# Query, key and value projections on scaled fp16 halves instead of float32r halves, in a gated mix of memory attention and a SiLU feed-forward

## The chip, the cores and the metric

The kernel runs on one core of one Trainium2 chip (trn2). The metric is the device time of one launch in microseconds (us); lower is better. Runs of one kernel are compared on the same chip.

## What is computed

`x` has 2048 rows of 448 features. Block A is attention with 16 heads of 28 features in four segments of 512 rows; each segment attends within itself and also reads a running memory of the earlier segments. Block B is a feed-forward of 1792 inner features. A gate per row mixes the two.

```python
q, k, v = x @ wq, x @ wk, x @ wv            # heads of 28, segments of 512 rows
phi = lambda t: where(t > 0, t + 1, exp(t))
for s in range(4):
    logits = qs @ ks.T * 28 ** -0.5 + mask  # masked where key > query: -1e9
    a_dot = softmax(logits) @ vs
    a_mem = (phi(qs) @ M) / (phi(qs) @ z + 1e-6)
    o[s] = g * a_mem + (1 - g) * a_dot      # g = sigmoid(beta), one per head
    M, z = M + phi(ks).T @ vs, z + phi(ks).sum()
a = o @ wo
b = silu(x @ w1) @ w2
out = sigmoid(x . gate_w) * a + (1 - sigmoid(x . gate_w)) * b
```

## The kernel before, in words

**Two parts for each number.** TensorE multiplies fewer bits than a float32 has, so each operand is split into a high part and a low remainder, and a product is the sum of high*high, high*low and low*high. `passes` lists these: 448 features are three chunks of 128 and a last one of 64, whose low part is packed beside the high, so 3*3 + 2 = 11 matmuls make one product. `product` (L547, matmuls at L555) runs them in groups of 3, 3, 3 and 2, one per chunk, into one PSUM bank. The q and k products of a segment and a group of four heads (`proj`, 16 of each) are 11 matmuls of 128x512; `vproj` (16, one per 128 rows) is 11 matmuls of 128x450 (448 and a column for the gate). That makes 176 matmuls for each of q, k and v.

**Which parts.** Before, q, k and v use float32r parts: the high part is a rounded copy (ScalarE, L770, L786, L810), the low part a plain subtraction (VectorE or GpSimd, L774, L791, L813). They need no scale. The feed-forward uses fp16 parts (`halves`, L512: ScalarE at L515, VectorE at L507), and these need a power-of-two scale, since fp16 has a small exponent range. So `x` is loaded twice: into `xraw` for the projections, whose float32r parts `xT` live in two buffers, and later into `rawf`, from which `x16` (L523) makes the fp16 parts `xh` for the feed-forward, segment 0 within stage one and the other three in stage two.

**Scales.** `size` (L379, VectorE) takes the largest magnitude of a loaded piece per partition. `scales(a, b)` turns several of these into a scale: a reduction (`most`, L405), a TensorE transpose (L409), four small VectorE steps (L412 to L416), a TensorE broadcast (L418) and two more VectorE steps that give `up`, the scale, and `top`, its inverse (L422, L423). Before, scales were needed only behind the projections, at the eviction of PSUM: `sqk` and `sv` scale q, k and v into fp16 pairs (`stg`, L846, L848; `vt`, L902, L906).

**phi.** From the PSUM of `proj`: `pr` = relu(-q) on ScalarE (L862), `pe` = exp(-pr) on ScalarE (L864), `ph` = max(q, 0) + pe on VectorE (L865), which reads PSUM again. For q, `phq` splits it in two float32r parts (L869, L871); for k it is transposed (L882) and becomes `phk` (L885, L887). `memory` (L936, L938) and `retrieve` (L973, L974) are the running memory.

**Stages and order.** Stage one is `project()`: it loads `x` and the weights, makes q, k, v, the memory parts and the scales of everything. When it ends, its SBUF is given to stage two, where attention (`maxima`, L660 and L670; `attention`, L1216 to L1258) is interleaved with the feed-forward (L555 on `xh,wa`, L1095 to L1118). At the end the output projection (L555 on `wos,oT`) is added.

No order is written out by hand. A list scheduler (`Sched`) holds a cost for each task, adds a hop time when a result goes from one engine to another (`HOP`), and in each step starts the task that can begin first; among equals the priority decides. What it settles is a fixed order per engine: each engine executes its own queue strictly in that order, and an instruction whose input is late holds up all behind it. Tasks with two possible engines (`either`, `scaled`) go to VectorE or GpSimd by their costs. All DMAs are issued from SP. PSUM has three banks for projections and feed-forward (`mm`), three for scores and v (`sc`) and two others (`cc`). `WARM` = 15 matmuls on a constant run first, while the first data is loaded.

Of the kernel before, what the change touches and what calls it, by code (L numbers as in the profile page):

```python
# [8 lines left out]
F32 = mybir.dt.float32  # L9
# [26 lines left out]
WARM = 15  # L36
BANKS = {"mm": 3, "sc": 3, "cc": 2}
# [7 lines left out]
WOT = 30.0  # L45
TUS = 1.6
TLAT = 4.0
SLACK = 0.75
LOP = 14.63
LATE = 0.08  # L50
FIRST = 120.0
WPRIO = 120.0
# [4 lines left out]
MP = 14.75  # L57
VF = 2.5
VA = 1.36
VS = 6.77  # L60
NV = 8
XS0 = 2.29
VC = -7.5
OT1 = 6.44
XS = 4.78
QS = -4.81
KS1 = -3.68
SS = -1.76
# [6 lines left out]
PRICE = 27.28  # L75
PVRUNS = [((1, 0), 1)]
PVP = 45.81
FLO = -17.93
FHI = 690.04
WOP = 96.32  # L80
SZ = 26.65
SZSTEP = 1.85
XPRIO = 81.97
WBP = -7.77
# [23 lines left out]
class Sched:  # L108
# [3 lines left out]
    HOP = {"PE": 0.2, "ACT": 0.145, "DVE": 0.13, "POOL": 0.1, "SP": 0.1}  # L112
# [124 lines left out]
def infini_mix(ctx: ExitStack, tc: tile.TileContext, x, wq, wk, wv, wo, beta, w1, w2, out):  # L237
# [67 lines left out]
    def scaled(cols, fn, *deps, **k):  # L305
        eng = {"DVE": nc.vector, "POOL": nc.gpsimd}
        return sch.add(("DVE", "POOL"), (0.07 + 0.00104 * cols, 0.2 + 0.0042 * cols), lambda e: fn(eng[e]), deps, port=True, **k)
# [35 lines left out]
    own2 = const.tile([128, 2], F32, name="own2")  # L343
    upw = const.tile([128, 3], F32, name="upw")
    sqk = const.tile([128, 2 * NSEG], F32, name="sqk")
# [4 lines left out]
    sv = const.tile([128, NSEG], F32, name="sv")  # L350
# [7 lines left out]
    X16 = {0: base.tile([128, 7, L], F16, name="xh0")}  # L358
# [11 lines left out]
    SIZE, SCALED, XH = {}, {}, {}  # L370

    def size(j, view, n, *deps, uses=(), prio):
# [8 lines left out]
        SIZE[j].append(dve(n, go, *deps, uses=uses, prio=prio))  # L381

# [7 lines left out]
    def scales(a, b, prio):  # L390
# [5 lines left out]
        wide1 = a <= W1 < b  # L396

        def m1():
            if wide1:
                for j in range(a, b):  # L400
                    nc.vector.tensor_reduce(most[:, j:j + 1], sizes[:, cols[j][0]:cols[j][1]], axis=AX.X, op=OP.max)
                for j in (HQ, HK):
                    nc.vector.tensor_max(most[:, W1:W1 + 1], most[:, W1:W1 + 1], most[:, j:j + 1])
            else:
                nc.vector.tensor_reduce(most[:, a:b], sizes[:, cols[a][0]:cols[b - 1][1]].rearrange("p (j n) -> p j n", j=n),  # L405
                                        axis=AX.X, op=OP.max)
        t = dve(500 if wide1 else 130, m1, *[d for j in range(a, b) for d in SIZE[j]],
                *([SCALED[HQ], SCALED[HK]] if wide1 else []), prio=prio)
# [114 lines left out]
    def x16(s, prio, *deps):  # L523
# [4 lines left out]
        for c in range(4):  # L528
            r = Buf(RAW)
            d = dma(262e3, lambda c=c, r=r: start(r.v, x[s, :, c]), *deps, takes=[r], prio=prio + 0.01 * c)  # L530
            if s == 0:
# [5 lines left out]
                def src(r=r):  # L537
                    return r.v.rearrange("p (c n) -> p c n", c=4)
# [867 lines left out]
```

## Time and profile before

| what | value |
|---|---|
| time, median of 3 runs | 576.42 us (575.96 to 577.6) |
| span of the profiled execution | 574.4 us |
| what lies around that span, against the median | 2.0 us |
| instructions | 11662 |
| TensorE busy | 556.2 us (97%), 4055 matmuls |
| VectorE busy | 426.7 us (74%) |
| ScalarE busy | 398.7 us (69%) |
| GpSimd busy | 346.3 us (60%) |
| DMA | 83.14 MB, mean 145 GB/s |
| mean granted TensorE clock | 0.991 |

The profile lists no time of its own for the profiled execution beside its span, so the 2.0 us between span and median are taken as a constant around it. A matmul's duration in the profile is its way through the array; matmuls overlap, so the rate is read from how far apart they start, and TensorE's 97% is not 97% of its peak.

### The profile page before, as it was taken

The numbers are of one execution on the slowest core, as the hardware profiler recorded it, in microseconds if no ns is written. First come the engines' busy times: TensorE is split into PE (matmuls) and PEld (weight loads), VectorE is DVE, ScalarE is ACT, GpSimd is POOL, SyncE is SP. The second block draws the span as 40 slices with busy tenths as digits, with TensorE's granted clock in tenths as the row PEclk, the third lists the DMA queues.
The fourth block names the chain that finished last, engine by engine and source line by source line (L and its number), as shares of the span: only waits on it lengthen the run. The fifth ranks groups of instructions, "written<-read, shape, count | busy, mean of one in ns | idle before, by whom it ended". The sixth has DMA issues, their size and how long they took to land.

```text
span 574.4 us, 11662 instructions
## 1 busy us (share of the span) xinstructions
PE 556.2 (97%) x4055; PEld 346.0 (60%) x4055; DVE 426.7 (74%) x1104; ACT 398.7 (69%) x695; POOL 346.3 (60%) x489
## 2 busy tenths in 40 slices
PE   9899999999998999999999999999999999999997
PEld 5587877888854455555565555555555654544544
DVE  7898889779877996578865688777996327555634
ACT  7568878566558788799977799967999846142321
POOL 5803626534324579999978899887999971131300
PEclk9899999999999799999999999999999999999999
DMA  8577875435747444344313433245330237888521
GB/s 302 181 231 224 249 206 168 130 99 165 238 127 199 127 144 146 98 119 109 96 53 110 136 104 99 64 154 141 109 87 4 64 113 242 209 235 236 130 77 65
DMA packets 80363, 83.14 MB, mean 145 GB/s; under 512 B 44296, under 2 KB 67976, under 8 KB 80304
## 3 DMA queue, kind: packets, MB, share of 16 engines
q1 hardware_dynamic: 80304, 82.39, 48.7%
q8 instruction: 32, 0.52, 0.4%
q14 instruction: 27, 0.22, 0.1%
HBM read 52.60 MB, written 26.09 MB: 137 GB/s over the span
## 4 chain that ended last, share of the span: by engine, by line
PE 56%; DVE 17%; ACT 10%; POOL 7%; DMA 5%; issue 5%; SPq 0%; DVEq 0%; ACTq 0%; POOLq 0%
PE mm L555 19%; PE mm L1118 16%; PE sc L555 8%; POOL phl L1237 4%; PE sc L1216 4%; PE sc L660 3%; DVE sc L670 3%; PE cc L1250 3%; ACT pf L1221 3%; DMA rawf<-in_w_dram 3%; ACT phl L1233 2%; DVE stg L848 2%; DVE ph L865 1%; DVE sizes L379 1%; DVE xh L507 1%
## 5 line engine op out<-in xcount | busy, mean ns | idle before, releaser
L1237 POOL TENSOR_TENSOR phl<-pf,phl 128x384 f16<-128x384 f32 (+1 forms) x192 | 190.2, 1013 | 12.2 <-ACT phl L1233 11.8
L1118 PE MATMUL mm<-wb,ghl 128*128 128x448 f16 (+1 forms) x684 | 143.4, 349 | 1.0 <-DVE ghl L1101 0.8
L555 PE MATMUL mm<-xh,wa 128*128 128x512 f16 x572 | 141.7, 379 | 0.5 <-DVE ghl L1101 0.4
L670 DVE CUSTOM_DVE_ANT_0 sc<-sc,mk 128x384 f32<-128x384 f32 (+1 forms) x192 | 105.1, 569 | 33.3 <-PE sc L660 26.1
L1221 ACT ACTIVATE pf<-sc,es 128x512 f32<-128x512 f32 (+1 forms) x192 | 109.4, 621 | 19.7 <-PE sc L1216 16.0
L1118 PEld LDWEIGHTS <-ghl 128*128 128x128 f16 x684 | 65.2, 97 | 57.0 <-issue 3.1
L555 PEld LDWEIGHTS <-wa 128*128 128x128 f16 x572 | 54.5, 97 | 57.8 <-issue 4.0
L1233 ACT ACTIVATE phl<-pf 128x1280 f16<-128x1280 f32 x64 | 81.5, 1275 | 10.7 <-POOL pf L1227 10.2
L660 PE MATMUL sc<-ring 84*128 84x128 f16 (+3 forms) x256 | 59.2, 304 | 2.7 <-DVE mx L670 1.7
L1216 PE MATMUL sc<-ring 86*128 86x512 f16 (+3 forms) x256 | 58.8, 302 | 2.2 <-ACT pf L1221 1.0
L1095 ACT ACTIVATE th<-mm,ths 128x512 f32<-128x512 f32 x52 | 35.7, 691 | 33.3 <-PE mm L555 33.3
L1097 DVE SCALAR_TENSOR_TENSOR mm<-th,mm 128x512 f32<-128x512 f32 x52 | 36.4, 705 | 19.4 <-ACT th L1095 19.3
L555 PE MATMUL mm<-xT,wqs 128*128 128x512 f32 x176 | 48.2, 409 | 0.1
L1250 PEld LDWEIGHTS <-phl 128*128 128x128 f16 x1280 | 42.1, 97 | 10.0 <-issue 1.3
L555 PE MATMUL mm<-xT,wks 128*128 128x512 f32 x176 | 45.7, 401 | 0.0
L1258 DVE TENSOR_REDUCE oraw<-cc 128x116 f32<-128x232 f32 x64 | 25.0, 392 | 26.1 <-PE cc L1250 25.9
L1250 PE MATMUL cc<-vg,phl 128*128 128x29 f16 (+1 forms) x1280 | 44.0, 183 | 0.0
L566 POOL TENSOR_TENSOR ol<-ol,ml 128x448 f32<-128x448 f32 x12 | 14.2, 1180 | 48.2 <-DMA ol<-o_scr 29.0
L1101 DVE SCALAR_TENSOR_TENSOR ghl<-mm,ghl 128x512 f16<-128x512 f32 x52 | 35.5, 685 | 9.4 <-ACT ghl L1099 9.1
L555 PE MATMUL sc<-wvs,xT 128*128 128x450 f32 x176 | 40.4, 375 | 0.2 <-DVE wvs L813 0.2
L1216 PEld LDWEIGHTS <-ring 86*128 86x128 f16 x256 | 24.1, 98 | 23.3 <-issue 4.7
L1099 ACT ACTIVATE ghl<-mm 128x512 f16<-128x512 f32 x52 | 30.8, 599 | 9.6 <-DVE mm L1097 9.6
(163 smaller groups left out, 903.6 us busy)
## 6 DMA issues: line engine op xcount, KB each, us to landing
rawf<-in_w_dram SPq DMA_DIRECT2D x26, 256.0 KB
rawf<-in_w_dram SPq DMA_DIRECT2D x28, 224.0 KB
xraw<-in_x_dram SPq DMA_DIRECT2D x16, 256.0 KB
rawf<-in_x_dram SPq DMA_DIRECT2D x16, 256.0 KB
v_scr<-vt SPq DMA_DIRECT2D x16, 232.0 KB
vg<-v_scr SPq DMA_DIRECT2D x16, 232.0 KB
q_scr<-stg SPq DMA_DIRECT2D x16, 224.0 KB
k_scr<-stg SPq DMA_DIRECT2D x16, 224.0 KB
```

Source lines behind the costliest of these rows:

```text
L555: nc.tensor.matmul(ps(), *p[i], start=(i == 0), stop=(i == n - 1))
L660: nc.tensor.matmul(ps.v[:, u:u + n], rg.v[:KS, 0, hh, i * 128:(i + 1) * 128], rg.v[:KS, 1, hh, :n], start=(i > 0), stop=(i > 0 or j == 3), ...
L670: nc.vector.tensor_tensor_reduce(r, r, MK[:, L - n:], 1.0, NEG, OP.add, OP.max, mx.v[:, hh, i:i + 1])
L1095: e1 = sact(L, lambda ps=ps, th=th: nc.scalar.activation(th.v, ps.v, AF.Tanh, scale=ths[:, s:s + 1]), m, takes=[th], uses=[ps], prio=p0)
L1097: e2 = dve(L, lambda ps=ps, th=th: nc.vector.scalar_tensor_tensor(ps.v, th.v, 1.0, ps.v, op0=OP.add, op1=OP.mult), e1, uses=[ps, th], prio=p0)
L1101: e4 = dve(L, lambda ps=ps, g=g: nc.vector.scalar_tensor_tensor(g.v[:, 1], ps.v, DOWN, g.v[:, 0], op0=OP.mult, op1=OP.subtract), e3, uses= ...
L1118: nc.tensor.matmul(ps.v[:, lo:hi], g.v[:, y, sl], w.v[:, z, lo:hi], start=(j == 0 and i == 0), stop=(j == len(fs) - 1 and i == 2))
L1216: nc.tensor.matmul(ps.v[:, e:e + w], rg.v[:KK, 1, hh, j * 128:(j + 1) * 128], rg.v[:KK, 0, hh, j * 128:], start=True, stop=True)
L1221: ex.append(sact(e, lambda b=b, ps=ps, pf=pf, e=e: nc.scalar.activation(pf.v[:, b, :e], ps.v[:, :e], AF.Exp, scale=es[:, s:s + 1]), m, *ex ...
L1233: hi = copy(1280, lambda hl=hl, flat=flat: nc.scalar.activation(hl.v[:, 0], flat(), AF.Copy), *mk, takes=[hl], uses=[pf], prio=p0 + 2)
L1237: low = pool(w - u, lambda hl=hl, flat=flat, u=u, w=w: nc.gpsimd.tensor_sub(hl.v[:, 1, u:w], flat()[:, u:w], hl.v[:, 0, u:w]), low, uses=[ ...
L1250: nc.tensor.matmul(p[:, i, :2 - z], hl.v[:, z, u:u + 128], vg.v[:, j, hh, :2 - z], start=(z == zs[0] and i == 0), stop=(z == zs[-1] and j ...
```

## The change

The q, k and v projections now use the fp16 parts of the feed-forward, so the scales of `x`, `wv`, `wq` and `wk` are needed before the first product. The parts of `x` are made once, in stage one, for all four segments (`xhalves` into `X16`, now in the base pool), and the feed-forward reads them; `x16` and its loads are gone. The sizes of the weights are now sums of squares on ScalarE (`squares`), and their scale is a power of two near the root. The product comes out scaled, so q, k and v are evicted with one constant (`FIT`); phi gets its scale from `tqk` and `nqk`; `pp` = max(q, 0) is a VectorE step of its own that reads PSUM, and `ph` = pp + pe is now an addition from SBUF that may go to either VectorE or GpSimd. 16 further warm-up matmuls (`MORE` pairs) are spread between the first scales. The ring `xraw` grows from 6 to 8 buffers. Some thirty costs and priorities of the scheduler are set anew. The core of the diff:

```diff
+MORE = 8
+HPRIO = -3.02
+FIT = 2.0 ** -26
-SLACK = 0.75
-LOP = 14.63
+SLACK = 0.94
+LOP = 17.33
...
-    HOP = {"PE": 0.2, "ACT": 0.145, "DVE": 0.13, "POOL": 0.1, "SP": 0.1}
+    HOP = {"PE": 0.29, "ACT": 0.235, "DVE": 0.22, "POOL": 0.19, "SP": 0.19}
...
-    X16 = {0: base.tile([128, 7, L], F16, name="xh0")}
+    X16 = {s: base.tile([128, 7, L], F16, name=f"xh{s}") for s in range(NSEG)}
...
+    def squares(j, view, n, *deps, uses=(), prio):
...
+        SIZE[j].append(copy(n + 200, lambda: nc.scalar.activation(junk.v[:, :n], view(), AF.Square, accum_out=sizes[:, lo:lo + 1]),
...
+            if root:
+                nc.vector.tensor_scalar(few[:, 2:3].bitcast(I32), few[:, 1:2].bitcast(I32), 1, 0x3f800000,
+                                        op0=OP.logical_shift_right, op1=OP.bitwise_and)
...
+    def true(s, prio):
+        def go():
+            for i, j in enumerate((WQ, WK)):
+                nc.vector.tensor_scalar(tqk[:, 3 * s + i:3 * s + i + 1], top[:, j:j + 1], top[:, xi(s)], None, op0=OP.mult)
+            nc.vector.tensor_scalar(nqk[:, 3 * s:3 * s + 2], tqk[:, 3 * s:3 * s + 2], -1.0, None, op0=OP.mult)
...
-    def x16(s, prio, *deps):
...
-        XTR = cycle([wp.tile([128, 7, L], F32R, name=f"xT{i}") for i in range(2)])
-        W = {n: wp.tile([128, 8, D + 2 if n == "v" else L], F32R, name=f"w{n}s") for n in "qkv"}
+        W = {n: wp.tile([128, 8, D + 2 if n == "v" else L], F16, name=f"w{n}s") for n in "qkv"}
...
-        ring("xraw", [128, L], F32, 6)
+        ring("xraw", [128, L], F32, 8)
+        ring("pp", [GW, L], F32, 2)
...
+        for _ in range(MORE):
+            END1.append(pe(half(L, 2), lambda: [nc.tensor.matmul(
+                wb.v, maskb, maskb[:, None, :].to_broadcast([128, 4, 128]), start=True, stop=True) for _ in range(2)],
+                END1[-1], uses=[wb], prio=200))
...
-        def xquarter(tb, prio):
...
-        def xfeat(s, c, prio):
...
+        def xhalves(s, c, prio):
...
+            XC[s, c] = halves(NSEG - 1 - s, hi, lo, lambda: X16[s], src, L, d, prio, uses=[b])
+            XH.setdefault(s, []).extend(XC[s, c])
...
+                squares(j, v, n, d, uses=[b], prio=prio + 0.01 * c)
                 if name != "v":
...
+                    size(j + 1, lambda v=v: v().rearrange("p (g e) -> p g e", g=NG)[:, :, GW:], 64, d, uses=[b],
+                         prio=HPRIO + 0.01 * c)
...
+        def whalves(name, prio):
...
+                WS[name][c] = halves(j, (ALL, c), [((ALL, 4 + c), (ALL,), (ALL, c))], lambda: W[name], v, n, d, prio + 0.01 * c,
+                                     uses=[b], more=SIZE[j + 1][c:c + 1] if name != "v" else [])
...
-            p = product(lambda: ps.v, lambda: passes(w, XT[s].v), L, prio,
-                        deps={c: WS[which][c] + (XC[s, c] if s else XDONE[0]) for c in range(NC + 1)}, takes=[ps],
-                        uses=[XT[s]])
+            p = product(lambda: ps.v, lambda: passes(w, X16[s]), L, prio,
+                        deps={c: WS[which][c] + (XC[s, c] if s else XH[0]) for c in range(NC + 1)}, takes=[ps],
+                        kind=half)
...
-            hi = sact(L, lambda: nc.scalar.activation(hl.v[:, 0], ps.v, AF.Copy, scale=sqk[:, k:k + 1]), p,
-                     (QREADY if which == "q" else KREADY)[s], takes=[hl], uses=[ps], prio=prio)
+            hi = act(L, lambda: nc.scalar.activation(hl.v[:, 0], ps.v, AF.Copy, scale=FIT), p, takes=[hl], uses=[ps],
+                     prio=prio)
...
-            tp = dve(L, lambda: nc.vector.scalar_tensor_tensor(ph.v, ps.v[:GW], 0.0, e.v, op0=OP.max, op1=OP.add), te,
-                     takes=[ph], uses=[e, ps], prio=prio)
+            tu = dve(L, lambda: nc.vector.tensor_scalar(po.v, ps.v[:GW], tk, 0.0, op0=OP.mult, op1=OP.max), p, QREADY[s],
+                     takes=[po], uses=[ps], prio=prio)
+            te = copy(L + 65, lambda: nc.scalar.activation(e.v, r.v, AF.Exp, scale=nqk[:GW, k:k + 1]), tr, QREADY[s], takes=[e],
+                      uses=[r], prio=prio)
+            tp = either(L, lambda g: g.tensor_add(ph.v, po.v, e.v), te, tu, takes=[ph], uses=[e, po], prio=prio)
...
         for tb in range(TB):
-            load_x(0, tb, -9 + 0.01 * tb + (0.5 if tb else 0))
-        weight("v", wv, -8.9, places[:4])
+            load_x(0, tb, -12 + 0.01 * tb)
+        weight("v", wv, -11, places[:4])
+        weight("q", wq, -10, places[4:8])
+        weight("k", wk, -9, places[8:])
+        t_gh = gates()
+        scales(NSEG - 1, NSEG, -12)
         for tb in range(TB):
-            xquarter(tb, -9 + 0.01 * tb + (0.5 if tb else 0))
...
+            xhalves(0, tb, -11.5 + tb * 0.7 + (tb > 0))
+        scales(WV, WV + 1, -11)
+        whalves("v", -10.8)
+        scales(WQ, WQ + 1, QS)
+        whalves("q", QS + 0.1)
+        scales(WK, WK + 1, KS1)
+        whalves("k", KS1 + 0.1)
...
-            if s not in XH:
-                x16(s, prio(0) - XLEAD, *list(t1.values())[:1])
```

The retrieve products (L973, L974) keep their float32r parts. The size of the columns of `wq` and `wk` that hold a block of `w1` (`HQ`, `HK`) stays on VectorE, one small reduction for each loaded piece.

More of the change, by code (lines that the diff above doesn't have):

```diff
@@ L1044, in project @@
         END1.append(scales(W1, W2 + 1, WPRIO - 10))
-        x16(0, XPRIO, SCALED[W1])
-        END1.extend(XH[0])
+        for s in range(NSEG):
+            DER[s] = derive(s, XPRIO + s)
+            END1.append(DER[s])
         END1.extend(GDONE)
```

317 lines of the change are left out of this document (131 added, 186 removed).

## The prediction, made before the changed kernel ran

> **What bounds the kernel now.** I read the page first (span, busy shares, slices), then the busy times by stage, then the instructions in order of time and in groups.
>
> ```profile
> span 574.4 us, 11662 instructions
> PE 556.2 (97%) x4055; PEld 346.0 (60%) x4055; DVE 426.7 (74%) x1104; ACT 398.7 (69%) x695; POOL 346.3 (60%) x489
> PEclk9899999999999799999999999999999999999999
> ```
>
> TensorE (PE) is busy almost throughout, so a microsecond is won only if TensorE issues fewer or faster matmuls or waits less. The windows split this by stage (columns: length, busy time of PE, weight loads, VectorE, ScalarE, GpSimd, then granted clock, DMA share, GB/s):
>
> ```profile
> 0.00:6.00 6.00, 4.96 (x14) 1.88 (x15) 2.62 (x11) 3.27 (x5) 3.97 (x25) 1.00 0.66 211
> 6.00:14.00 8.00, 7.81 (x36) 6.20 (x35) 7.18 (x14) 6.45 (x12) 3.71 (x4) 1.00 1.01 367
> 14.00:18.60 4.60, 1.94 (x10) 1.29 (x9) 4.50 (x13) 2.81 (x8) 4.60 (x4) 1.00 0.77 261
> 18.60:22.10 3.50, 3.50 (x11) 2.33 (x10) 3.50 (x14) 1.62 (x4) 3.50 (x4) 0.51 0.65 227
> 22.10:30.00 7.90, 7.90 (x38) 6.20 (x37) 6.16 (x26) 4.06 (x10) 4.26 (x4) 1.00 0.37 124
> 30.00:60.00 30.00, 29.76 (x156) 24.69 (x155) 27.48 (x81) 23.78 (x54) 5.90 (x8) 1.00 0.80 237
> 60.00:163.60 103.60, 99.78 (x560) 83.08 (x559) 87.92 (x216) 72.35 (x157) 45.50 (x74) 1.00 0.58 172
> 163.60:200.00 36.40, 34.10 (x192) 16.50 (x192) 31.48 (x86) 26.03 (x43) 15.27 (x21) 0.91 0.55 154
> 200.00:570.00 370.00, 365.81 (x3048) 203.44 (x3047) 255.09 (x649) 258.35 (x410) 259.62 (x350) 1.00 0.42 122
> ```
>
> Stage one ends at 163.6. From 30 on TensorE stands idle only 0.24 + 3.82 = 4.1 us of it; in the change of stage 2.3; in the remaining 370 us 4.2. The clock of 0.91 there is about 6.6 us at half rate (0.09 * 36.4 / 0.5). VectorE is full from 14 to 22 and busy 115.4 of 133.6 us (86%) from 30 to 163.6: it is the second bound of stage one. So the change can win by the matmul rate, a little by stalls, and can lose at the start.
>
> **Part a, the matmul rate.** Rows in order of time, of runs without a gap, and the two weight loads:
>
> ```profile
> 28.78 4.17 PE L555 MATMUL sc<-wvs,xT 128*128 128x450 f32 x19
> 32.79 2.68 PE L555 MATMUL mm<-xT,wks 128*128 128x512 f32 x11
> 163.63 11.70 PE L555 MATMUL mm<-xh,wa 128*128 128x512 f16 x53
> 484.57 8.49 PE L555 MATMUL sc<-wos,oT 128*128 128x448 f16 x44
> L555 PE MATMUL mm<-xT,wks 128*128 128x512 f32 x176 | 45.7, 401 | 0.0
> L555 PEld LDWEIGHTS mm<-xT,wks 128*128 128x128 f32 x176 | 33.1, 192 | 6.7
> L555 PEld LDWEIGHTS <-wa 128*128 128x128 f16 x572 | 54.5, 97 | 57.8 <-issue 4.0
> ```
>
> A run of n lasts n-1 intervals and one matmul's way (0.35 to 0.40 us). Float32r, 512 columns: (2.68-0.40)/10 = 0.228; fp16: (11.70-0.38)/52 = 0.218. Float32r, 450 columns: (4.17-0.38)/18 = 0.211; fp16, 448 columns: (8.49-0.35)/43 = 0.189, taken as 0.190 for 450. The count of matmuls is the same. By 28.78 the kernel before has issued 75 of the 528, as the order of its instructions shows (33 of 512, 42 of 450); the other 319 and 134 gain 319*0.010 + 134*0.021 = 3.2 + 2.8 = 6.0 us. **a = -6.0.**
>
> **Part b, the start.** The first 75 are compared by their time of arrival. Before, v starts at 6.04, since its parts need no scale:
>
> ```profile
> 3.77 0.63 ACT L770 ACTIVATE xT<-xraw 128x512 fp32r<-128x512 f32 x1 [1.69 <-DMA xraw<-in_x_dram]
> 6.04 2.82 PE L555 MATMUL sc<-wvs,xT 128*128 128x450 f32 x10
> 7.75 0.58 ACT L810 ACTIVATE wvs<-raw 128x450 fp32r<-128x450 f32 x1 [1.38 <-DMA raw<-in_wv_dram]
> 7.75 2.31 SPq L313 DMA_DIRECT2D wa<-in_wk_dram  x4
> 17.21 0.15 DVE L405 TENSOR_REDUCE most<-sizes 128x2 f32<-128x8 f32 x1
> 17.93 0.27 DVE L412 TENSOR_REDUCE few<-cc 2x1 f32<-2x128 f32 x1
> 19.67 0.13 DVE L423 COPY top<-cc 128x2 f32<-128x2 f32 x1
> L379 DVE TENSOR_REDUCE sizes<-xraw 128x1 f32<-128x512 f32 x16 | 10.5, 675 | 0.0
> L387 ACT ACTIVATE rawf<-rawf 128x512 f32<-128x512 f32 x13 | 8.2, 627 | 0.2 <-DMA rawf<-in_w_dram 0.2
> L387 ACT ACTIVATION_READ_ACCUMULATOR rawf<-rawf 128x1 f32 x27 | 5.2, 194 | 0.0
> L515 ACT ACTIVATE xh<-rawf,up 128x512 f16<-128x512 f32 x16 | 11.3, 718 | 2.0 <-DMA rawf<-in_x_dram 2.0
> L507 DVE SCALAR_TENSOR_TENSOR xh<-rawf,up,xh 128x384 f16<-128x384 f32 x4 | 2.5, 621 | 0.0
> L507 DVE SCALAR_TENSOR_TENSOR wa<-rawf,up,wa 128x512 f16<-128x512 f32 x13 | 9.9, 770 | 2.4 <-ACT wa L515 2.4
> ```
>
> The first load is there at 3.7, the fifth at 7.7, and later ones follow every 0.66 ((2.31-0.33)/3: SP issues the next when an old one has landed). With the changed order x lands from 3.7 to 5.8, `wv` 7.7 to 9.7, `wq` 10.3 to 12.2, `wk` 12.9 to 14.8. A scale takes 2.6 us from `most` to `top` (17.21 to 19.80). I follow the queues of the changed kernel as built:
> - VectorE: four x sizes at 0.675, `most` at 7.2, the four small steps to 8.8. Ahead of x's reciprocal the queue has the small size of the first `wq` piece (lands 10.3), `most` of v (after four squares of 0.63 + 0.19 on ScalarE, 11.0) and the size of the second piece. So x's scale is there at 11.6, not at 9.8.
> - ScalarE: squares of v to 11.0, two of q to 12.6, the high part of x's first quarter to 13.3, two squares to 14.9, then `wv` high at 0.65 each. VectorE makes the low parts behind it at 0.7: 16.3 for the first chunk of `wv`, 18.7 for the last; then x's second and third quarter to 20.6.
> - TensorE: v0 from 16.3 to 19.1, v1 to 21.8, v2 to 23.9. The steps for q's scale stand behind those low parts on VectorE: scale at 23.2, `wq` high from 23.5, its low chunks from 25.8 to 28.2 at 0.8. q0 runs from 25.9 to 28.7.
>
> At 28.7 that is 44 matmuls (33 v, 11 q) where the kernel before had 75, so it is behind by 22 of 512 and 9 of 450: 22*0.218 + 9*0.190 = 6.5. **b = +6.5**, with bounds +2 (if x's scale is there at 9.8 and nothing stands ahead) and +10 (if each low part waits for GpSimd as well). A half clock like that at 18.6 (0.51, 11 matmuls in 3.5 us) is likely at v0, after TensorE's idle time; v0 to v2 would end about 1 us later and still ahead of q0's first part at 25.8, which hides it.
>
> **Part c, stalls of stage one after that.** Evictions no longer wait for a scale, and a PSUM bank is released after two evictions, one relu and one max; the exp and the addition have left its chain (0.63 and 0.68 below).
>
> ```profile
> L864 ACT ACTIVATE pe<-pr 112x512 f32<-112x512 f32 x24 | 15.1, 630 | 0.5
> L865 DVE SCALAR_TENSOR_TENSOR ph<-mm,pe 112x512 f32<-112x512 f32 x24 | 16.3, 680 | 2.1 <-ACT pe L864 2.1
> L871 POOL TENSOR_TENSOR phq<-ph,phq 112x512 fp32r<-112x512 f32 x8 | 10.3, 1290 | 9.1 <-ACT phq L869 9.1
> L507 DVE SCALAR_TENSOR_TENSOR xh<-rawf,up,xh 128x512 f16<-128x512 f32 x9 | 7.4, 844 | 0.0
> ```
>
> 22 of the 24 additions go to GpSimd, some 1.29 each: the chain to `phk` and `phq` grows by about 0.6, but those feed the memory products, which the queue has some microseconds later. I take three quarters of the 4.1 us idle: **c = -3.0**, bounds -4.1 and, if VectorE becomes the bound, +7 (first rival).
>
> **Part d, stage two.** Gone are 12 of the 16 `xh` rounds: 12*0.72 on ScalarE, 12*0.84 on VectorE and 12 loads of 256 KB. TensorE's work hides nearly all of that, so its worth is bounded by the idle time, 2.3 + 4.2, and by the half clock. I take half of the idle: **d = -3.0**, bounds +3 (another interleaving) and -9. Sum: -6.0 + 6.5 - 3.0 - 3.0 = -5.5, on the profile's 574.4 + 2.0, that is 576.4 - 5.5 = **570.9 us**.
>
> **The rivals.** First, slower: VectorE becomes the bound of stage one.
>
> ```profile
> L379 DVE TENSOR_REDUCE sizes<-raw 128x1 f32<-128x448 f32 x4 | 2.4, 602 | 0.0
> L813 DVE TENSOR_TENSOR wvs<-raw,wvs 128x450 fp32r<-128x450 f32 x4 | 2.5, 622 | 0.6 <-ACT wvs L810 0.6
> L774 DVE TENSOR_TENSOR xT<-xraw,xT 128x384 fp32r<-128x384 f32 x4 | 2.2, 559 | 2.5 <-ACT xT L770 2.4
> L456 DVE TENSOR_SCALAR sqk<-upw,up 128x1 f32<-128x1 f32 x4 | 0.8, 202 | 0.0
> ```
>
> Gone are the 24 `ph` (16.3), the sizes of 12 weight pieces (near 0.58: 7.0), float32r low parts (`wvs`, `xT` and its last chunk, four `phq`: 8.7) and some 18 small steps at 0.2 (3.6); added are 24 `pp` (as `ph`, 16.3), two additions (1.4), 12 low parts of weights at 0.80, ten of `xh` at 0.84, and small steps and one more scale (4.3): 40.0 against 35.6. The 139.4 us of the windows up to 163.6 become 143.8, of which about 22 lie before 28.7. At 86% busy the other 121.8 take 141 us and stage one ends at 169.7; with d that is 576.4 + 6.1 - 3.0 = 579.5. It decides if VectorE can't be kept above 121.8/137.9 = 88%. For it: the 86%. Against: 27.48 of 30 us (92%) from 30 to 60, and later TensorE, not VectorE, was full. My forecast needs 92%. Chance 0.20.
>
> Second, the shared port. The low parts (two SBUF inputs) could wait for GpSimd's additions, which also read SBUF: 22 new ones, GpSimd busy about half of the time, half of 1.29 each: 7.1 us on VectorE and then on TensorE, 578.0. The rows of such steps show no sign of it: 0.84 for 512 columns is what 0.62 for 384 makes (0.62*512/384 = 0.83). Chance 0.04. The Trainium skill (SBUF — State Buffer, "Who interferes with whom") says that such a pair holds one port exclusively and the later one blocks; by that rule this is the case to fear.
>
> Third, no gain in rate: a matmul's interval depends on its columns alone, and the 0.228 comes from something that stays. Then a = 0 and the time is 576.9. Chance 0.05: the two float32r rows and the two fp16 rows agree with each other. The Trainium skill (TensorE: Matmul & The Clock Gate, "Back-to-back issue gap") gives columns/2.4 + 2.5 ns with no term for the type, 216 ns for 512; the fp16 row fits it, the float32r row doesn't.
>
> Fourth, faster: the new order closes most gaps. b = +3, c = -4.1, d = -9: 576.4 - 16.1 = 560.3. For it: the idle time and half clock of the change of stage; against: the queues at the start as followed above. Chance 0.15.
>
> **How the numbers follow.** The forecast has 0.56, within 565 to 574.5 by its own bounds. A measurement can tell about 0.3% (1.7 us) from no change. Faster: forecast and fourth, 0.71. Same: second and third, 0.09. Slower: first, 0.20. From 558 to 581 about half of the first and of the fourth rival's tails, some 0.16, is left out.
>
> **What would show it.** Right: float32r's 190 ns loads gone from q, k and v, runs of 11 at 0.216 to 0.218; first v matmul at 15 to 17 us and first q near 26; last stage-one matmul at 160 to 162; VectorE over 90% busy from 30 on. Wrong: first q before 22 (b too large), stage one past 164 with TensorE waiting for VectorE's `pp`, `stg` or low parts (first rival), or a stretch from the end of stage one to the last matmul that is not 404 us (now 407) within 4.

## The result and the profile after

The changed kernel takes **567.96 us** (567.26 to 570.33, four runs) against 576.19 us (575.93 to 577.6, four runs) of the kernel before on the same chip: ratio **0.986**, 95% interval 0.9835 to 0.9887. It is faster by 8.2 us, within the forecast of 570.9 us (558 to 581).

The head of its page; its PEclk line is 9 in every slice, where before one slice was 7 and one 8:

```profile
span 565.5 us, 11682 instructions
PE 545.0 (96%) x4073; PEld 299.9 (53%) x4073; DVE 422.2 (75%) x1093; ACT 397.4 (70%) x703; POOL 362.9 (64%) x504
PEclk9999999999999999999999999999999999999999
```

The windows of before and after, cut at 28.78 and at the end of stage one, which is now 161.9 (columns: length, busy time of PE, weight loads, VectorE, ScalarE, GpSimd, then granted clock, DMA share, GB/s). First before, then after:

```profile
28.78:163.80 135.02, 130.96 (x721) 109.05 (x721) 116.78 (x302) 96.83 (x210) 51.40 (x81) 1.00 0.63 186
163.80:203.80 40.00, 37.70 (x227) 18.50 (x226) 35.08 (x96) 29.06 (x49) 17.48 (x23) 0.91 0.56 158
203.80:570.60 366.80, 362.61 (x3015) 201.68 (x3013) 251.29 (x639) 255.13 (x404) 257.41 (x347) 1.00 0.42 121
```

```profile
28.78:161.90 133.12, 126.52 (x740) 71.85 (x739) 120.79 (x318) 100.13 (x216) 83.86 (x107) 1.00 0.60 178
161.90:201.90 40.00, 37.92 (x240) 18.45 (x239) 35.63 (x83) 29.87 (x49) 18.89 (x24) 1.00 0.58 161
201.90:561.80 359.90, 357.64 (x3000) 200.25 (x2999) 243.10 (x627) 247.90 (x390) 256.00 (x348) 1.00 0.42 115
```

Stage one ends 1.9 us earlier (161.9 against 163.8), and the stretch from there to the last matmul is 399.9 against 406.9: 7.0 us shorter. Together they are the 8.9 us between the spans. In the second stretch TensorE's idle time fell from 2.30 + 4.19 to 2.08 + 2.26, and the half clock (0.91 of 40 us; the clock record has it for 6.8 us, which costs 3.4) is gone in this execution. The mean granted clock of the four executions is 1.000, 0.997, 1.000 and 0.996, so two of them have 3 to 5 us of half clock somewhere (an estimate: the missing share times the span, doubled). In stage one the idle time did not fall, it rose: 4.06 to 6.60 us.

TensorE at the start, in order of time:

```profile
14.77 0.35 PE L539 MATMUL sc<-wvs,xh 128*128 128x450 f16 x1
15.38 3.86 PE L539 MATMUL sc<-wvs,xh 128*128 128x450 f16 x19 [0.26 <-DVE wvs L515]
20.10 2.65 PE L539 MATMUL sc<-wvs,xh 128*128 128x450 f16 x13
22.58 0.38 PE L539 MATMUL mm<-xh,wqs 128*128 128x512 f16 x1
23.72 2.55 PE L539 MATMUL mm<-xh,wqs 128*128 128x512 f16 x11 [0.76 <-DVE wqs L515]
26.24 2.27 PE L539 MATMUL sc<-wvs,xh 128*128 128x450 f16 x11
28.35 0.59 PE L539 MATMUL mm<-xh,wqs 128*128 128x512 f16 x2
```

By 28.78 that is 44 matmuls of v and 14 of q. What TensorE waited for from 28.78 to the end of stage one (total, times, longest), before and then after:

```profile
PE cc L418 <- DVE diag L416: 0.8, 2, 0.6
PE cc L973 <- ACT phq L869: 0.8, 1, 0.8
PE sc L882 <- DVE mx L670: 0.7, 1, 0.7
PE cc L974 <- DVE phq L871: 0.4, 1, 0.4
PE cc L974 <- POOL phq L871: 0.3, 1, 0.3
PE sc L882 <- DVE ph L865: 0.3, 1, 0.3
PE cc L938 <- DVE phk L887: 0.2, 1, 0.2
```

```profile
PE cc L949 <- POOL phq L847: 2.5, 3, 1.2
PE sc L644 <- DVE phk L863: 1.5, 1, 1.5
PE sc L539 <- DVE vt L881: 1.1, 1, 1.1
PE sc L858 <- POOL ph L842: 0.2, 1, 0.2
```

Before, no single wait is over 0.8 us, and the waits that end in `ph`, `phq` or `phk` make 2.0 us (1.5 of them for phq, spread over three engines). After, these make 4.2 us: the retrieval (L949) waits 2.5 us for GpSimd's low part of phq, and 1.5 us go to one PSUM bank that is released only by `phk`. The chain to phq now goes through GpSimd twice, for the addition `ph` and for the low part.

### The profile page after: what moved, and what is told of

The parts are those of the page before. It is cut to its first block, busy times and chain, and to the rows that moved or that the text cites. A ratio compares the mean times of both kernels' runs of the same rounds, so it can differ in the third digit from the quotient of the medians.

```text
span 565.5 us, 11682 instructions
## 1 busy us (share of the span) xinstructions
PE 545.0 (96%) x4073; PEld 299.9 (53%) x4073; DVE 422.2 (75%) x1093; ACT 397.4 (70%) x703; POOL 362.9 (64%) x504
## 4 chain that ended last, share of the span: by engine, by line
PE 71%; DVE 15%; POOL 4%; issue 3%; DMA 3%; ACT 3%; SPq 0%; DVEq 0%; POOLq 0%; ACTq 0%
PE mm L539 25%; PE mm L1094 20%; PE sc L539 7%; PE sc L1190 6%; PE cc L1224 5%; PE sc L644 5%; DVE sc L654 3%; DVE stg L821 1%; DVE pp L836 1%; POOL ph L842 1%; DVE xh L515 1%; DVE wb L515 1%; DMA raw<-in_wq_dram 1%; POOL phq L847 1%; DMA xraw<-in_x_dram 1%
## 5 line engine op out<-in xcount | busy, mean ns | idle before, releaser
L1094 PE MATMUL mm<-wb,ghl 128*128 128x448 f16 (+1 forms) x684 | 146.8, 349 | 2.1 <-DVE ghl L1077 1.6
L644 PE MATMUL sc<-ring 84*128 84x128 f16 (+3 forms) x256 | 57.0, 299 | 1.8 <-DVE phk L863 1.5
L1071 ACT ACTIVATE th<-mm,ths 128x512 f32<-128x512 f32 x52 | 36.0, 694 | 20.9 <-PE mm L539 20.8
L539 PE MATMUL mm<-xh,wqs 128*128 128x512 f16 x176 | 43.3, 379 | 0.8 <-DVE wqs L515 0.8
L539 PE MATMUL mm<-xh,wks 128*128 128x512 f16 x176 | 42.6, 379 | 0.0
L539 PE MATMUL sc<-wvs,xh 128*128 128x450 f16 x176 | 37.0, 353 | 1.4 <-DVE vt L881 1.1
L842 POOL TENSOR_TENSOR ph<-pp,pe 112x512 f32<-112x512 f32 x22 | 28.3, 1288 | 15.6 <-ACT pe L840 7.8
```

The lines of the kernel that those rows point to most:

```text
L539: nc.tensor.matmul(ps(), *p[i], start=(i == 0), stop=(i == n - 1))
L644: nc.tensor.matmul(ps.v[:, u:u + n], rg.v[:KS, 0, hh, i * 128:(i + 1) * 128], rg.v[:KS, 1, hh, :n], start=(i > 0), stop=(i > 0 or j == 3), ...
L1071: e1 = sact(L, lambda ps=ps, th=th: nc.scalar.activation(th.v, ps.v, AF.Tanh, scale=ths[:, s:s + 1]), m, takes=[th], uses=[ps], prio=p0)
L1094: nc.tensor.matmul(ps.v[:, lo:hi], g.v[:, y, sl], w.v[:, z, lo:hi], start=(j == 0 and i == 0), stop=(j == len(fs) - 1 and i == 2))
```

## The experiments

The twelve runs are timed in five rounds beside the kernel before (574.96 to 575.62 us in these groups). The trace of each gives the end of stage one and the stretch from there to the last matmul, with TensorE's idle time in the stretch and the time for which the clock record shows half rate in it. "Durations" are the costs and hop times given to the scheduler, "priorities" the nine constants of stage two (WOT, SLACK, LOP, PRICE, PVP, FLO, FHI, WOP, WBP).

| run | us | ratio (95%) | stage one ends | stretch | idle | half clock |
|---|---|---|---|---|---|---|
| before | 576.19 | 1 | 163.8 | 406.9 | 6.5 | 6.8 |
| after | 567.96 | 0.986 (0.9835-0.9887) | 161.9 | 399.9 | 4.3 | 0 |
| x1_redo | 605.87 | 1.051 (1.0485-1.0543) | 163.2 | 438.3 | 20.9 | 41.0 |
| x2_oldsched | 579.60 | 1.009 (1.0056-1.0116) | 165.8 | 407.6 | 6.9 | 10.2 |
| x3_newsched | 583.54 | 1.014 (1.0119-1.0158) | 159.9 | 418.1 | 11.0 | 17.1 |
| x4_phq_dve | 568.87 | 0.988 (0.9863-0.9901) | 162.4 | 401.0 | 4.4 | 1.9 |
| y1_redo_w2first | 585.86 | 1.018 (1.0163-1.0189) | 162.5 | 417.9 | 11.5 | 23.9 |
| y2_oldcosts | 660.63 | 1.148 (1.1458-1.1495) | 167.7 | 488.2 | 35.1 | 132 |
| y3_oldprio2 | 571.93 | 0.994 (0.992-0.9954) | 161.3 | 404.4 | 6.6 | 3.4 |
| y4_xsize_act | 567.97 | 0.986 (0.9847-0.9876) | 162.1 | 400.9 | 4.4 | 2.0 |
| z1_start | 576.93 | 1.003 (1.0016-1.0045) | 168.0 | 404.6 | 7.7 | 3.4 |
| z2_before_durations | 580.66 | 1.011 (1.0078-1.0149) | 161.7 | 411.1 | 9.2 | 10.2 |
| z3_start_sizes_phq | 568.20 | 0.988 (0.9856-0.9903) | 163.5 | 399.6 | 4.4 | 0 |
| z4_start_sizes_phq | 569.95 | 0.991 (0.9882-0.9936) | 160.8 | 403.4 | 6.6 | 3.4 |

Stretch minus idle minus half of the half-clock time is 394 to 399 us in every row but y2. The work of stage two is thus about the same in all of them, and what differs is how often TensorE stands, and how long its clock is half.

### x1: sharing taken away

```diff
+            if s and s not in XH2:
+                x16(s, prio(0) - XLEAD, *list(t1.values())[:1])
...
-                    ... L, p0, deps=wd + PREV,
+                    ... L, p0, deps=wd + XH2.get(s, []) + PREV,
```

Here `x16` loads x again and makes its fp16 parts again in place.

> The changed kernel, but in stage two x of segments 1 to 3 is loaded again through the two rawf buffers and its fp16 parts are made again in place before the feed-forward reads them, as often as in the kernel before (12 loads, 12 ScalarE and 12 VectorE steps). What is in dispute: from the end of stage one to the last matmul the change won 7.0 us (407.1 to 400.1), 3.0 were forecast. If the shared parts of x brought that (the two buffers, VectorE and ScalarE are free in the change of stage), this kernel loses 5 to 7 us: 573 to 575 us, and the stretch is 405 to 407. If the scheduler's new costs and priorities brought it, the time stays within 1.5 us of 568 and the stretch is 400 to 401.5.

Measured 605.87 us, far over both expectations. The windows of 202 to 302 us, after and then x1:

```profile
202.00:302.00 100.00, 99.59 (x938) 57.95 (x938) 73.32 (x216) 83.24 (x129) 93.03 (x131) 1.00 0.34 96
202.00:302.00 100.00, 83.53 (x613) 42.69 (x612) 55.44 (x153) 62.69 (x97) 78.31 (x103) 0.80 0.33 94
```

TensorE issues 613 matmuls instead of 938, at a clock of 0.80. The w2 pieces share two load buffers with the remade x, and their ten low parts start at 184 to 281 us (after: 183 to 219); the second segment's feed-forward starts at 290.7 (after: 234.4). With no feed-forward matmuls to fill in, TensorE waits for each step of attention. Sharing x's parts is worth 38 us under this schedule, far from what 24 instructions and 12 loads cost by themselves.

### x2 and x3: the schedule, with and without the new parts

x2 is the changed kernel with the old durations and the nine old priorities; x3 is the kernel before with the new ones. Of x2's edit, one of the nine priorities and the hop times (the durations of single tasks are left out):

```diff
-WBP = 7.74
+WBP = -7.77
...
-    HOP = {"PE": 0.29, "ACT": 0.235, "DVE": 0.22, "POOL": 0.19, "SP": 0.19}
+    HOP = {"PE": 0.2, "ACT": 0.145, "DVE": 0.13, "POOL": 0.1, "SP": 0.1}
```

> The changed kernel with the scheduler's former hop times, the former costs of the attention tasks and of the low parts, and the former priorities of stage two (WOT, SLACK, LOP, PRICE, PVP, FLO, FHI, WOP, WBP). If the new schedule brought the 7.0 us of stage two: 573 to 576 us, stretch from the end of stage one to the last matmul 405 to 408. If the shared parts of x brought it: 567 to 570 us, stretch 400 to 402; stage one may shift by 2 us either way, as the hop times count there too.

> The kernel before with the scheduler's new hop times, new costs of the attention tasks and low parts, and the new priorities of stage two; projections and x as before. If the new schedule brought the 7.0 us: 569 to 572 us, stretch from the end of stage one to the last matmul 400 to 402 instead of 407.1. If the shared parts of x brought it: 575 to 578 us, stretch 405 to 408. If the half clock of 6.8 us in the change of stage was chance of one execution, the stretch is some 3 us shorter and neither is shown.

Measured 579.60 and 583.54 us, each outside both of its expectations: either half of the change by itself is slower than the kernel before. "The parts" stand here for all of the change but these durations and nine priorities. In stage one they cost 2.0 us under both schedules (163.8 to 165.8, 159.9 to 161.9), and the new schedule brings 3.9 us with both kinds of parts. In the stretch behind, the parts alone change little (406.9 to 407.6), the schedule alone loses 11 us (418.1), and both together win 7.0.

The idle time of TensorE from 28.78 to the end of stage one goes with the parts, not with the schedule: 4.1 to 7.4 us under the old one (before, x2), 2.7 to 6.6 under the new one (x3, after). So do the waits of 0.2 us and more that end in `ph`, `phq` or `phk`: 2.0 to 3.6 and 1.7 to 4.2.

### x4: phq's low parts on VectorE

```diff
-            b = either(L, lambda e: e.tensor_sub(h2.v[:, 1], ph.v, raw(h2.v[:, 0])), a, uses=[ph, h2],
+            b = dve(L, lambda: nc.vector.tensor_sub(h2.v[:, 1], ph.v, raw(h2.v[:, 0])), a, port=True, uses=[ph, h2],
```

> The changed kernel with the low part of phq always on VectorE (0.69 us) and never on GpSimd (1.29 us). In the changed kernel TensorE waits 2.5 us for GpSimd's phq low part in three places, which the kernel before hardly did. If GpSimd's longer chain (addition 1.29, then low part 1.29) is what ate the forecast gain of stage one: those waits go, stage one ends 1.5 to 2.5 us earlier (159.2 to 160.2), time 565.5 to 566.5. If VectorE (91% busy from 22 us on) is the bound there: its 12 further steps of 0.69 cost TensorE other waits, stage one ends at 161.7 to 165 and the time is 568 to 571.

Measured 568.87 us, no gain. The scheduler also moved six of the 22 additions from GpSimd to VectorE. The window of 60 to 161 us, after and then x4, and x4's first wait of TensorE from 22 to 162:

```profile
60.00:161.00 101.00, 94.54 (x563) 54.84 (x561) 89.64 (x224) 71.91 (x157) 73.24 (x97) 1.00 0.56 164
60.00:161.00 101.00, 95.22 (x561) 54.84 (x560) 98.06 (x247) 73.02 (x157) 48.92 (x75) 1.00 0.54 163
```

```profile
PE cc L949 <- DVE phq L847: 2.4, 4, 1.8
```

GpSimd lost 24 us of work, VectorE gained 8 and was 97% busy, and stage one ended 0.5 us later; it should have ended 1.5 to 2.5 us earlier if the two steps on GpSimd had eaten the gain. The clock was half for 3.4 us from 160.9; the 1.5 us of that in stage one cost 0.7, so without it stage one would have ended about as in the changed kernel. The wait for phq went along to the other engine.

### y1: w2 ahead of the remade x

x1 with one priority set back:

```diff
-WBP = 7.74
+WBP = -7.77
```

> The changed kernel with the parts of x of segments 1 to 3 loaded and made again in stage two (as in the run that did only that: 605.9 us), but with the kernel before's priority for the w2 weights, so that these stand ahead of the remade x in the two load buffers they share. Theory (the late w2 pieces starve TensorE): w2's parts are there by about 215 as in the changed kernel, the feed-forward of the second segment starts before 260, the half-clock windows go, and most of the 38 us come back: 570 to 582 us. Rival (the remake itself is the cost: loads, 24 more instructions, segment by segment late): the parts of x come later still, the second segment's feed-forward stays behind 280, and the time stays above 595 us.

Measured 585.86 us, between the two. The second segment's feed-forward starts at 258.8, before 260 as the theory had it, and 20 us come back. But the clock is half for 23.9 us from 229.7, and 18 us stay. The test was not clean: nine of w2's ten low parts start by 213, but the tenth piece stands behind the first four remade pieces of x in the load buffers. Its rows, and TensorE's behind it:

```profile
242.85 0.34 SPq L316 DMA_DIRECT2D rawf<-in_w_dram  x1
248.58 1.03 POOL L518 TENSOR_TENSOR wb<-rawf,wb 128x448 f16<-128x448 f32 x1
249.16 9.79 PE L1094 MATMUL mm<-wb,ghl 128*128 128x448 f16 x39
258.79 1.46 PE L539 MATMUL mm<-xh,wa 128*128 128x512 f16 x6
```

In TensorE's order 39 matmuls on w2 stand between the tenth piece and the second segment. In each of the four runs that lose most, the second segment starts 9 to 10 us behind the tenth low part; in before, after and x2 it starts 15 to 35 us behind, so the piece does not hold it up there.

| run | tenth low part of w2 starts | second segment's feed-forward starts |
|---|---|---|
| before | 210.6 | 242.4 |
| after | 219.0 | 234.4 |
| x2_oldsched | 213.8 | 248.9 |
| x3_newsched | 246.2 | 255.0 |
| y1_redo_w2first | 248.6 | 258.8 |
| x1_redo | 280.8 | 290.7 |
| y2_oldcosts | 371.2 | 380.8 |

So a late last piece of w2 is in x1, x3, y1 and y2 what the second segment waits behind. How much of x1's loss would stay with all ten pieces first is not shown.

### y2 and y3: durations and priorities apart

Both are the changed kernel; y2 has x2's edit of the durations alone, y3 that of the nine priorities alone. Of y2 the hop times, then of y3 one priority:

```diff
-    HOP = {"PE": 0.29, "ACT": 0.235, "DVE": 0.22, "POOL": 0.19, "SP": 0.19}
+    HOP = {"PE": 0.2, "ACT": 0.145, "DVE": 0.13, "POOL": 0.1, "SP": 0.1}
...
-WOT = 50.57
+WOT = 30.0
```

> The changed kernel with only the kernel before's durations and hop times in the scheduler; all priorities are the new ones. With these and the old stage-two priorities together it took 579.6 us (stage one to 165.8, then 407.6 us to the last matmul). Theory: the durations order stage one, the priorities order stage two; so stage one ends near 165 to 166 and the rest stays near 400 to 402: 570 to 574 us. Rival: the durations make both (the scheduler's idea of how long a result takes decides the interleaving everywhere): 166 and 406 to 408, 578 to 580 us.

> The changed kernel with only the kernel before's nine priorities of stage two (WOT, SLACK, LOP, PRICE, PVP, FLO, FHI, WOP, WBP); durations and stage-one priorities are the new ones. Theory: stage one ends as in the changed kernel, 161 to 163, and the stretch behind it goes from 399.9 to 404 to 408 us, with w2's parts earlier and half-clock windows again in the change of stage: 572 to 577 us. Rival: the durations make the gain, the priorities do little: 161 to 163 and 399 to 402, 567 to 570 us.

y2 fell outside both expectations: 660.63 us. Its lines of PE and clock:

```profile
PE   7989999899999787878887899999999999999997
PEclk8989999999879976565555799999999999999999
```

New priorities on old durations leave TensorE short of work from 250 to 360 us; the second segment's feed-forward starts at 380.8. y3 took 571.93 us, just under the theory's 572 to 577: stage one about as in the changed kernel, 404.4 behind it, with a half clock of 3.4 us at 194.9. So with shared parts the durations are worth 4.5 us in stage one and 3.2 behind (x2 to y3), and the priorities another 4.5 behind (y3 to after), but only on top of the durations: without them (y2) the same priorities bring w2's tenth part to 371.2.

### y4: the sizes of x on ScalarE

```diff
-            size(NSEG - 1 - s, lambda: b.v, L, d, uses=[b], prio=prio + (XS if s else XS0))
+            if s:
+                squares(NSEG - 1 - s, lambda: b.v, L, d, uses=[b], prio=prio + XS)
+            else:
+                size(NSEG - 1, lambda: b.v, L, d, uses=[b], prio=prio + XS0)
-        root = a in (WV, WQ, WK)
+        root = a in (WV, WQ, WK) or a < NSEG - 1
```

> The changed kernel with the sizes of x of segments 1 to 3 (12 reductions of 0.67 us on VectorE, 8.1 us) made as sums of squares on ScalarE (12 of 0.83 us), which is what the change does for the weights; their scale is then the root's power of two. Theory (VectorE, 91% busy from 22 to 161.7, holds up stage one, and the waits for GpSimd's phq are its reflection): the idle time of TensorE in stage one falls from 7.4 to 3 to 5 us, stage one ends at 157.5 to 160, and the time is 564 to 566 us. Rival (the chains to phq and phk are long by the number of steps in them, not by VectorE's load): stage one ends at 161 to 163, 567 to 570 us, with VectorE some 5% less busy there.

Measured 567.97 us, as the rival had it. VectorE is at 86.51 of 101 us in the same window, 3 less, and TensorE's idle time from 22 on fell from 7.4 to 5.4; stage one still ended at 162.1. The clock fell to half at 160.7, which cost 0.7 us of it; v0 came 0.55 later, but by 28.78 that was made up (42 matmuls of v and 17 of q, against 44 and 14). The rest lies in TensorE's busy time behind 28.78, 127.9 us against 126.5 for two matmuls fewer, and was not traced further. VectorE at 86% or 97%: the end of stage one moves by 0.5 us.

### z1: VectorE's queue at the start

```diff
-        scales(WQ, WQ + 1, QS)
+        scales(WQ, WQ + 1, -12)
...
-                    size(j + 1, ..., 64, d, uses=[b],
+                    size(j + 1, ..., 64, d, SCALED.get(NSEG - 1), uses=[b],
...
-            size(NSEG - 1 - s, lambda: b.v, L, d, uses=[b], prio=prio + (XS if s else XS0))
+            size(NSEG - 1 - s, lambda: b.v, L, d, *([w for c in WS["q"].values() for w in c] if s == 1 else []), uses=[b], ...)
```

> The changed kernel with VectorE's queue at the start in another order: wq's small sizes behind the scale of x, the scale of wq ahead of wv's last low parts and x's last quarters (now it comes behind them, at 19.1 to 21.1), and the sizes of the next segment of x (1.93 us) behind wq's low parts. Theory (the order of VectorE's queue sets the start, and a lost microsecond there passes to the end of stage one, since TensorE bounds it): v0 at 14.5 to 15, q0 at 20 to 21 instead of 22.6, stage one ends 1.5 to 2.5 us earlier, 159.5 to 160.5, and the time is 565.5 to 567 us if the rest stays at 400. Rival (the start is given back: what comes in later waits for VectorE instead): q0 earlier but stage one at 161 to 162.5, 567 to 569 us.

Measured 576.93 us, over both expectations. It did not test what it was for: with VectorE's queue fuller at that moment, the scheduler gave one of wv's low parts to GpSimd, which took two steps for it.

```profile
15.72 1.43 POOL L517 TENSOR_SCALAR raw<-raw,up 128x450 f32<-128x450 f32 x1 [1.77 <-ACT wvs L523]
17.24 1.36 POOL L518 TENSOR_TENSOR wvs<-raw,wvs 128x450 f16<-128x450 f32 x1
```

v0 waited 1.3 us for it, the clock was half for 6.8 us from 15.1, and q0 started at 25.8 instead of 22.6. A second half-clock time at 134.6 was not explained.

### z2: the kernel before with the new durations

```diff
-    HOP = {"PE": 0.2, "ACT": 0.145, "DVE": 0.13, "POOL": 0.1, "SP": 0.1}
+    HOP = {"PE": 0.29, "ACT": 0.235, "DVE": 0.22, "POOL": 0.19, "SP": 0.19}
```

> The kernel before with only the new durations and hop times; projections, parts of x and all priorities are the old ones. Theory (the durations alone bring stage one forward by about 4 us with either kind of parts: 163.8 to 159.9 with the new priorities of stage two as well, 165.8 to 161.9 with fp16 parts): stage one ends at 159 to 161. Behind it the parts of x and of w2 keep the old priorities, so the stretch stays at 404 to 410: 570 to 575 us. Rival (the gain of 3.9 was owed to the priorities, or the durations without shared parts upset stage two as they did with the new priorities, 418): over 578 us.

Measured 580.66 us (578.25 to 584.83, the profile is of the fastest execution), over the theory's 570 to 575 and within the rival's over 578. Stage one ended at 161.7, 2.1 us earlier, short of the expected 159 to 161; behind it the stretch grew from 406.9 to 411.1. Durations that help the changed kernel in both stages help this one in the first alone.

### z3 and z4: three edits together

z3 joins z1, x4 and y4. z4 adds, and puts wk's loads behind wq's parts:

```diff
+        if j in (WV, WQ, NSEG - 1):
+            return [h, dve(n + 64 * (len(lo) - 1), lambda: low(nc.vector), h, ...)]
...
-                squares(j, v, n, d, uses=[b], prio=prio + 0.01 * c)
+                squares(j, v, n, d, *([w[0] for w in WS["q"].values()] if name == "k" else []), uses=[b], prio=prio + 0.01 * c)
```

> The changed kernel with three edits together: the queue at the start as in the run with that alone, the sizes of x of segments 1 to 3 as squares on ScalarE, and phq's low parts always on VectorE. Theory (in stage one TensorE waits for chains of steps, each short; taking load from VectorE and the slow steps from GpSimd together shortens them, where one alone only moved the wait): TensorE's idle time after 22 falls from 7.4 to 2 to 4 us, stage one ends at 157 to 159.5, and the time is 562 to 565.5 us. Rival (the idle time is made by the scheduler's order and comes back whatever is taken away): stage one at 160 to 162, 566 to 569 us.

> As the run with the three edits together (568.2 us; there a low part of wv had moved to GpSimd, v0 waited 1.5 us for it, the clock was half for 6.8 us from 17.0, q0 came at 26.7, and TensorE had done 2.9 us less of the projections by 28.78 than the changed kernel; from 22 on it was idle 4.1 us instead of 7.4), and the low parts of wv, wq and x's first segment are kept on VectorE, and wk's squares stand behind wq's high parts on ScalarE. Theory (TensorE bounds stage one, so its end is the sum of the start's lag and the later idle time): v0 at 14.5 to 15.5, q0 at 20.5 to 22, no lag against the changed kernel at 28.78, idle time from 22 on 3 to 5 us, stage one ends at 157.5 to 160, and with 399 to 401 behind it the time is 563 to 567 us: about 2 to 5 us less than the changed kernel. Rival (what is won in stage one is lost in a new interleaving): stage one at 161 to 163 or a stretch over 402, 567 to 572 us.

z3 took 568.20 us, over the theory's 562 to 565.5. Its start was as bad as z1's (q0 at 26.7), but from 22 on TensorE was idle only 4.1 us, and stage one ended just 1.6 later than the changed kernel's. z4 mended the start only in part: q0 at 22.95 instead of 20.5 to 22, 0.6 us of projections ahead of the changed kernel by 28.78. With an idle time of 4.6 behind 28.78, against 6.6, stage one ended at 160.8, 1.1 earlier (2.6 us were due by those two numbers; the rest lies in TensorE's busy time, 127.4 us against 126.5 for three matmuls fewer, and was not traced further), and the stretch behind was 403.4, with 3.4 us of half clock at 195.5. The rival of z4 held: 569.95 us. No version beat the changed kernel.

## Why the prediction was right, and where not

The total was within 3 us, and that is in part luck: of its terms a, b and d came out better than forecast by 10.0 us together and c worse by 6.6, and one source, the schedule, was not in the sum at all. One of its own signs of being wrong did come, by a hair: the stretch behind stage one is 399.9, where 404 within 4 was named.

| term | forecast | measured |
|---|---|---|
| a, matmul rate | -6.0 | -9.2 |
| b, start | +6.5 | +3.7 |
| c, stalls of stage one | -3.0 | +3.6 |
| d, stage two | -3.0 | -7.0 |
| sum | -5.5 | -8.9 (span) |

**a held, mis-sized.** The median interval from one matmul to the next of its kind, behind 28.78, fell from 227 to 216 ns (512 columns) and from 205 to 190 (450): 319*0.011 + 134*0.015 = 5.5 us. On top come long intervals: before, 31 of 284 between q and k products and 7 of 121 within v took 270 to 430 ns, in all 3.7 us over the median; after, there is none. The working took its rates from single rows of runs without a gap and so missed most of these. The third rival (no gain in rate) is out. The weight loads show the type:

```profile
L539 PEld LDWEIGHTS <-wks 128*128 128x128 f16 x176 | 16.5, 98 | 16.8
```

**b held in kind, mis-sized.** x's scale came at 11.45 (11.6 forecast), behind wq's small sizes as said. But the squares on ScalarE follow each other every 0.6 us, where the sum had 0.63 + 0.19, so the high parts of wv begin at 13.90 and not at 14.9; and the low parts were faster than taken (rows of ScalarE and VectorE: start, length for all of the row):

```profile
7.99 0.58 ACT L389 ACTIVATE junk<-raw 128x450 bf16<-128x450 f32 x1 [5.92 <-DMA raw<-in_wv_dram]
8.56 0.56 ACT L389 ACTIVATE junk<-raw 128x450 bf16<-128x450 f32 x1
13.90 2.35 ACT L523 ACTIVATE wvs<-raw,up 128x450 f16<-128x450 f32 x4 [0.18 <-DVE up L434]
14.65 2.47 DVE L515 SCALAR_TENSOR_TENSOR wvs<-raw,up,wvs 128x450 f16<-128x450 f32 x4
22.91 1.41 DVE L515 SCALAR_TENSOR_TENSOR wqs<-raw,up,wqs 128x512 f16<-128x512 f32 x2
```

In a row the low parts take 0.62 and 0.70 each, where the sum had 0.7 and 0.8. v0 started at 14.77 instead of 16.3, and q0 was done by 26.24 instead of 28.7. The lag at 28.78 is 19 matmuls of 512 less 2 of 450: 19*0.216 - 2*0.190 = 3.7. The half clock forecast for v0 did not come in the changed kernel; it came in z1 and z3, where v0 had to wait, and in x4, for 3.4 us from 14.1.

**c failed.** 161.9 - 163.8 = -1.9 = -9.2 + 3.7 + c gives c = +3.6; TensorE's idle time says +2.5 of it. The other 1.1 lies in busy time of matmuls that the sum did not price, and was not traced. The step that failed is "those feed the memory products, which the queue has some microseconds later". The waits that end in `ph`, `phq` or `phk` rose from 2.0 to 4.2 us, which is 2.2 of the 2.5; and x2 and x3 show that they come with the parts under either schedule. In most places the queue does leave the time, but in three it doesn't, and the bank that waits for `phk` is a fourth. That the addition's 1.29 us on GpSimd is what makes these chains late is argued: no run put all additions back on VectorE. x4 moved the low part and six additions there and y4 took load from VectorE; in x4, y4, z3 and z4 a wait of 2.0 to 2.7 us for phq stayed, on whichever engine made it. z3 and z4, with both, brought the idle time from 22 on to 4.1 and 4.6 us from 7.4. This speaks for the chain through several loaded engines, not for one of them; whether its order or its length decides was not settled.

**The first rival is out, with its premise.** It let VectorE be the bound from 88% on; x4 ran it at 97% with stage one 0.5 us later.

**The second rival's mechanism is there, its price is not.** The prediction said that rows show no sign of it, and read this from a mean. The 0.84 of the nine `xh` rows is a mean of 739 to 1495 ns with a median of 742, so the kernel before showed it already. In both traces steps with two SBUF inputs are stretched when a subtraction or addition of GpSimd is still running as they start; steps that read PSUM are not (VectorE, after; min/median/max in ns):

```profile
L515 DVE SCALAR_TENSOR_TENSOR wa<-rawf,up,wa x11: 741/845/1697, 146.2 to 449.4; 128x512 f16<-128x512 f32 x11
L821 DVE SCALAR_TENSOR_TENSOR stg<-mm,stg x32: 628/681/693, 30.9 to 161.5; 128x512 f16<-128x512 f32 x32
```

Of the steps of 128x512 and 128x448 on `wa`, `xh` and `wb`, 23 in the two traces began while such a GpSimd step had 188 to 1147 ns still to run. Each lasted longer than its usual 744 or 677 ns by this remainder less 191 to 199 ns: with 1147 left it took 1697, with 298 left 845, with 188 left 741. A GpSimd subtraction or addition that began 78 ns or more behind the VectorE step added nothing to it. In x4 and z4 one VectorE step each kept its length, and there GpSimd's step is the long one: 1.29 us where its kind takes 0.22, and 1.42 where its kind takes 0.43. The trace agrees with the Trainium skill (SBUF — State Buffer, "Who interferes with whom") that a VectorE step with two SBUF inputs contends with a GpSimd step that reads SBUF. But in stage one only 4 such steps were stretched, by 2.6 us in all against the rival's 7.1, and on an engine that did not set the end.

**d was right in sign, too small, and its cause was not the one given.** "Half of the idle" was a guess between bounds. Measured: 2.2 us less idle, 3.4 less by the half clock (in the profiled execution), 1.4 not found. The prediction laid it to the work of the 12 `xh` rounds that is gone. x2, without that work but with the old schedule, has 407.6, as before; x3, with the new schedule but that work, 418.1. The gain needs both. One half of why is shown: without shared parts the new schedule brings w2's tenth part to 246.2 (x3) instead of 219.0, and the second segment waits behind it. The other half is not: w2's tenth part is no later in x2 than in the changed kernel, and why the new schedule spares the changed kernel the 10.2 us of half clock that x2 has from 188.6 was not traced. The prediction gave the schedule no term, and by x2 the new parts with the old schedule would have been slower than before by 0.9%. Stage one ends 2.0 us later there: -9.2 by the rate, +3.3 by the start (17 matmuls of 512 less 2 of 450) and so +7.9 by the rest, of which 3.3 are idle time, 1.7 a half clock of 3.4 us from 41.8, and 2.9 are not found.

**The fourth rival** (560.3) had b = +3 and d = -9 nearer to the truth (+3.7 and -7.0) and failed on c (-4.1, measured +3.6).

## What to carry to other kernels

Where one engine is full, a new format is worth what its rate saves only if the chains that feed that engine stay as short; here the later start and longer waits gave back 7.3 of 9.2 us in stage one. In a scheduled interleaving, price the schedule as a term of its own and test the data change and the schedule crosswise (four kernels): here each alone was slower and both together faster, so judging either by itself would have rejected it. And look at who shares a load buffer: transfers that are hidden by themselves can still push later ones, and one late piece then holds up all that stands behind it in a fixed order. Read a step's spread before its mean: a mean of 844 ns with a median of 742 was the contention that the prediction looked for.

## What the runs showed that was not expected

- With 512 columns a float32r stream is slower than its weight load explains. The next load starts 3 ns after a matmul, takes 188, and the next matmul follows 37 later (227, against fp16's 216), though the load ended 25 ns before an fp16 matmul would have started. With 450 columns the matmul follows 14 ns behind the load (205, against 190); there the load ends 1 ns after that, so it may set the interval. The cause stays open.
- In 28 of the 31 long intervals of q and k the weight load started 58 to 192 ns after the matmul, mostly 85, where in the others it starts within 3; the other three hold a second load. fp16 loads of 98 ns show no interval over 229.
- In x1's second stretch the half clock doubled the price of standing: 20.9 us of idle time came with 41.0 us at half rate, which cost about as much again. In y1 it was 11.5 us with 23.9.
